# Attention with MLP on one core: the last 64 queries of all heads in one group of 128x64 column tiles per batch

## The chip, the cores and the metric

The kernel runs on one core of a Trainium2 chip. The metric is the device time of one execution in microseconds (us). TensorE is called PE, its weight loads PEld, VectorE DVE, ScalarE ACT, GpSimd POOL and SyncE SP, as in the profile.

## What is computed

Eight batches of eight heads with 576 tokens of width 64 go through causal attention with a decay that the gates s give, and the result, 512 wide, through a normalised two-layer MLP with a residual:

```python
cum = np.cumsum(np.maximum(s, 0.0), axis=-1)
bias = -(cum[:, :, :, None] - cum[:, :, None, :])
scores = np.where(causal, -1e9, scale * q @ k.T + np.minimum(bias, 0.0))
attn = softmax(scores)
x = (attn @ v).transpose(0, 2, 1, 3).reshape(B, S, H * D)
out = x + np.maximum(layer_norm(x) * g_ln @ w_ch1, 0.0) @ w_ch2
```

The inputs are float32, q, k and v of shape (8, 8, 576, 64); the weights are 512x2048 and 2048x512.

## The kernel before

The 576 tokens of a batch are four full blocks of 128 and a tail of 64 (`NF` = 4, `NT` = 5, `TL` = 64). Batches 0 and 1 run in an older form. From batch 2 on the work goes in pairs of heads, n = 4 b + j for batch b and pair j, and it is made of steps, each a short function:

- `burst(n)` (step `B2`, L541): the scores of two heads, transposed (keys in partitions, queries in columns). A head's q and k have 64 rows, so the two heads lie in the upper and the lower half of PE's rows and their matmuls alternate. Each head fills three banks of 512 columns: sa (key block 0, queries 0 to 511), sb (key block 0 with the tail queries, then key block 1), sc (key blocks 2 and 3). The six banks come from the PSUM pool "s" (six banks).
- `burst_exp` (`bx`, L551) on ACT takes the exponential of a bank into `er`, which has four slots, so heads h and h + 4 share one. `burst_mask` (`bm`, L560) on POOL zeroes the diagonal blocks. `tails`, `tails_exp`, `tails_mask` (`sd`, `se`, `sm`) make the scores of the tail's keys with the tail's queries of all eight heads of a batch, into `ed`; the tail's keys lie in `kz`.
- `pv_two(n, i)` (`Y`, L613): the product with v of one head. For each of five query blocks t the key blocks kb up to t are summed, which is 1 + 2 + 3 + 4 + 5 = 15 matmuls with 128x128 weights from `er` (or `ed` for the tail's keys) and 66 columns of v (64, and two with the weights of the sums). The tail has 64 queries, but its weights are 128 columns wide too, offset so that the 64 land in the lower half of the partitions in even batches and in the upper half in odd ones. The result `pot` takes a bank of the pool "m", which has two and also holds the MLP's `py`.
- `norm_two(n, i)` (`K`, L639) on DVE: sums, reciprocal, multiplication of the four full blocks into `xb`, and of the tail's 64 rows into `xm`, where the tails of two batches share a tile.
- `u` and `U`: quarters of the MLP of earlier batches, four matmuls of 512 columns each (`ph`, L761, and `py`, L780). `ga`, `la`, `La`, `Da` are the normalisation; `cr`, `lr`, `lv`, `tr`, `vm`, `vo` load and prepare q, k and v of later batches, the casts and weightings on POOL. The tails of all batches go through the MLP at the very end, as four mixed tiles of 128 rows.

The order of all steps on all engines is written out by hand, in a table of words (`PLAN`, L1278), such as `Y.19.0 B2.20`: each engine does its instructions in the order in which the words issue them. Waits between engines follow from who writes and reads what. A pool's bank is given to the next user in the order of the words, and the first instruction of that user waits until the last reader of the bank is done. Where PE's instructions wait, that stands at the weight load or the matmul, and all that follows on PE stands behind it.

The start matters in one place: POOL clears parts of `er` (L915) and then issues the loads of batch 1's v (L191), for which PE waits.

Of the kernel before, what the change touches and what calls it, by code (L numbers as in the profile page):

```python
# [9 lines left out]
F32 = mybir.dt.float32  # L10
# [6 lines left out]
P = 128  # L17
# [13 lines left out]
def fast_path(  # L31
# [26 lines left out]
    EW = 1664  # L58
# [7 lines left out]
    ET = H * TL + 2 * TL  # L66
# [50 lines left out]
    kz = const.tile([P, H * TL + TL], BF16, name="kz")  # L117
# [9 lines left out]
    ed = [c3f[:, i * ET : (i + 1) * ET] for i in range(2)]  # L127
    c_hi, c_mid, c_lo = (c3[0:BH, j, :] for j in range(3))
# [347 lines left out]
    def side_scores(b, j, i, banks):  # L476
# [51 lines left out]
    def ed_rows(b):  # L528
        return ed[b % 2][0:TL, TL : TL * (1 + H)].rearrange("p (h c) -> p h c", c=TL)
# [9 lines left out]
    BANKS = (("sa", 0, 0), ("sa", 1, 0), ("sb", 0, OB), ("sb", 1, OB), ("sc", 0, OC), ("sc", 1, OC))  # L539
# [11 lines left out]
    def burst_exp(n, x):  # L551
        name, i, o = BANKS[x]
        nc.scalar.activation(  # L553
            out=er[:, 2 * n % 4 + i, o : o + 512],
            in_=bank["B", n].pop((name, i)),
            func=ACT.Exp,
            scale=scale,
        )

    def burst_mask(n, x):  # L560
        o, step = ((0, OB + 64), (OC, 320))[x // 2]
# [30 lines left out]
    def pv_norm(b, h):  # L592
# [15 lines left out]
    TAIL_TWO = (  # L608
        (OB, OC - 64, OC + 256, OC + 448),
        (OB - 64, OC - 128, OC + 192, OC + 384),  # L610
    )

    def pv_two(n, i):  # L613
# [4 lines left out]
        pot = ptile("m", [P, NT, D2], "pot")  # L618
        for t in range(NT):
            for kb in range(t + 1):  # L620
                if kb == NF:
                    o = (h + 1 - b % 2) * TL
                    cols = ed[b % 2][:, o : o + P]
                else:
                    o = KOFF[kb] + t * P if t < NF else TAIL_TWO[b % 2][kb]
                    cols = e[:, o : o + P]
                nc.tensor.matmul(  # L627
                    pot[:, t, :],
                    lhsT=cols,
# [9 lines left out]
    def norm_two(n, i):  # L639
        b, h = n // NJ, 2 * (n % NJ) + i  # L640
        pot = pots.pop((n, i))
        rinv = rinvs[:, b, h, :]
        sums = small.tile([P, NT], F32, name="sums", tag="sums")
        nc.vector.tensor_reduce(out=sums, in_=pot[:, :, D:D2], axis=AX.X, op=ALU.add)  # L644
        nc.vector.reciprocal(out=rinv, in_=sums)
        hs = slice(h * D, (h + 1) * D)
        nc.vector.tensor_tensor(  # L647
            out=xb[b][:, :, hs],
            in0=pot[:, 0:NF, 0:D],
            in1=rinv[:, 0:NF].unsqueeze(2).to_broadcast([P, NF, D]),  # L650
            op=ALU.mult,
        )
        pr = tail_rows(b)
        nc.vector.tensor_scalar_mul(
# [921 lines left out]
```

## Time and profile before

| | us |
|---|---|
| median of 3 runs | 345.16 |
| runs | 344.2 to 345.6 |
| span of the profiled execution | 343.7 |
| PE busy in it | 333.9 |
| DVE, ACT, POOL busy | 207.1, 186.8, 168.7 |

The profile is of one execution. Its span runs from the first to the last instruction on record; the runs' times are taken around the whole execution, so that their median is 1.5 us above that span. A time of the profiled execution other than its span is not given. In the lists of groups a row names the source line, the engine, the operation, output and inputs with their shapes, the count, then behind the bar the busy time in us, the mean duration of one in ns, and the idle time before it with what ended it. In the timeline a row begins with the start and the length in us; rows of the same kind that follow each other are merged, and x14 is their number. A matmul's length is its latency (0.19 us for 66 columns); what it takes PE is the distance between two starts.

### The profile page before, as it was taken

The page shows a single profiled execution, that of the slowest core. Times are in us where ns is not written, and L with a number is a line of the kernel's source. Part 1 is how long each engine was busy: PE and PEld are TensorE (multiplying, and loading weights), DVE is VectorE, ACT ScalarE, POOL GpSimd, SP SyncE. Part 2 cuts the span into 40 slices and gives each one's busy share as a digit, 9 for nine tenths or more (in the row PEclk, how much of TensorE's full clock was granted, in tenths as well). Part 3 has the DMA queues.
Part 4 walks back from the last instruction along what each step waited for, and adds up shares of the span by engine and source line. Part 5 has one row for each costly group of instructions (what it writes and reads, how often), then busy time and mean ns, then how long its engine had stood idle before and what let it go on. Part 6 is the DMA issues. An engine that isn't in the chain of part 4 may idle for free.

```text
span 343.7 us, 8035 instructions
## 1 busy us (share of the span) xinstructions
PE 333.9 (97%) x3093; PEld 185.4 (54%) x3093; DVE 207.1 (60%) x589; ACT 186.8 (54%) x347; POOL 168.7 (49%) x306
## 2 busy tenths in 40 slices
PE   7999999899999999999999999999999999999994
PEld 2989765445545555555455555554555444444443
DVE  7688787937675787545753774557448624523412
ACT  4888899668755685448546864386344204202200
POOL 8997678876588766755684476441301001000000
PEclk9999999999999999999999999999999999999998
DMA  9999999799999999997687955600410141021022
GB/s 153 189 184 179 201 198 212 174 243 225 198 220 248 220 226 202 212 229 157 154 198 194 224 106 126 138 2 2 122 63 0 29 126 46 2 79 44 0 64 65
DMA packets 147962, 48.59 MB, mean 141 GB/s; under 512 B 135280, under 2 KB 143760, under 8 KB 147920
## 3 DMA queue, kind: packets, MB, share of 16 engines
q1 hardware_dynamic: 121856, 38.34, 51.4%
q0 software_dynamic: 24304, 8.92, 22.1%
q10 hardware_dynamic: 1760, 0.79, 0.9%
q8 instruction: 25, 0.41, 0.5%
q14 instruction: 17, 0.14, 0.1%
HBM read 37.11 MB, written 9.44 MB: 135 GB/s over the span
## 4 chain that ended last, share of the span: by engine, by line
PE 85%; POOL 7%; DVE 2%; DMA 2%; issue 1%; POOLq 0%
PE py L780 35%; PE ph L761 34%; PE pot L627 7%; DMA v_bf<-in_v_dram 2%; POOL v_bf L191 2%; PE sa L548 2%; POOL rowb L179 2%; PE sc L548 1%; PE sb L548 1%; PE pot L583 1%; DVE xn L710 1%; POOL w_bf L252 1%; POOL kq L910 1%; DVE yo L792 0%; DVE stats L669 0%
## 5 line engine op out<-in xcount | busy, mean ns | idle before, releaser
L780 PE MATMUL py<-w_bf,hT 128*128 128x512 bf16 (+2 forms) x608 | 130.9, 368 | 1.1 <-DVE yo L792 1.1
L761 PE MATMUL ph<-xT,w_bf 128*128 128x512 bf16 x480 | 109.8, 379 | 0.0
L752 ACT ACTIVATE hT<-ph 128x512 bf16<-128x512 f32 x102 | 61.2, 604 | 80.4 <-PE ph L761 78.8
L780 PEld LDWEIGHTS <-hT 128*128 128x128 bf16 x608 | 56.0, 98 | 61.4 <-issue 1.4
L761 PEld LDWEIGHTS <-w_bf 128*128 128x128 bf16 x544 | 51.0, 98 | 56.2
L492 POOL TENSOR_SCALAR_AFFINE_SELECT er<-er 128x256 bf16<-128x256 bf16 x96 | 37.5, 405 | 60.2 <-ACT er L553 45.1
L792 DVE SCALAR_TENSOR_TENSOR yo<-py,rstd,xb 128x512 f32<-128x512 f32 x32 | 24.0, 750 | 47.5 <-PE py L780 43.8
L553 ACT ACTIVATE er<-sb 128x512 bf16<-128x512 f32 x48 | 28.2, 609 | 21.7 <-PE sb L548 18.5
L750 DVE TENSOR_SCALAR hT<-ph 128x512 bf16<-128x512 f32 x34 | 23.4, 690 | 25.3 <-PE ph L761 24.6
L553 ACT ACTIVATE er<-sa 128x512 bf16<-128x512 f32 x48 | 28.6, 609 | 13.1 <-PE sa L548 10.2
L232 POOL TENSOR_TENSOR v_bf<-rowtmp,wt 128x512 bf16<-128x512 f32 (+1 forms) x30 | 33.8, 1134 | 2.8 <-DMA rowtmp<-in_v_dram 2.7
L553 ACT ACTIVATE er<-sc 128x512 bf16<-128x512 f32 x48 | 28.8, 613 | 5.4 <-PE sc L548 5.4
L627 PEld LDWEIGHTS <-er 128*128 128x128 bf16 x672 | 25.7, 97 | 9.5 <-issue 0.6
L627 PE MATMUL pot<-v_bf,er 128*128 128x66 bf16 x672 | 28.0, 193 | 0.0
L710 DVE SCALAR_TENSOR_TENSOR xn<-xb,mv,gb 128x512 bf16<-128x512 f32 x28 | 26.9, 960 | 1.0
L684 POOL TENSOR_TENSOR rstd<-rstd,mhalf 128x4 f32<-128x4 f32 (+1 forms) x8 | 8.8, 1094 | 36.9 <-DVE rstd L683 32.6
L644 DVE TENSOR_REDUCE sums<-pot 128x5 f32<-128x10 f32 x48 | 7.9, 165 | 30.0 <-PE pot L627 29.7
L669 DVE BATCH_NORM_STATS2 stats<-xb 128x6 f32<-128x128 f32 (+1 forms) x84 | 24.0, 323 | 0.4
L217 POOL CAST kq<-rowtmp 128x512 bf16<-128x512 f32 (+1 forms) x30 | 20.0, 681 | 6.3 <-DMA rowtmp<-in_k_dram 6.2
L647 DVE TENSOR_TENSOR xb<-pot,rinvs 128x256 f32<-128x256 f32 x48 | 20.4, 424 | 1.6
L548 PEld LDWEIGHTS <-kq 64*128 64x128 bf16 x360 | 11.2, 94 | 10.1 <-issue 4.7
L987 ACT ACTIVATE er<-st 128x512 bf16<-128x512 f32 x24 | 13.1, 603 | 1.8 <-PE st L978 1.8
(173 smaller groups left out, 398.3 us busy)
## 6 DMA issues: line engine op xcount, KB each, us to landing
out_dram<-yo SPq DMA_DIRECT2D x32, 256.0 KB
rowtmp<-in_v_dram SPq DMA_DIRECT2D x24, 256.0 KB
rowtmp<-in_k_dram SPq DMA_DIRECT2D x20, 256.0 KB
rowtmp<-in_q_dram SPq DMA_DIRECT2D x20, 256.0 KB
w_bf<-in_moe_w_ch_dram POOLq DMA_DIRECT2D x8, 512.0 KB, 9.2
kp<-in_k_dram POOLq DMA_DIRECT2D x8, 144.0 KB, 8.9
qp<-in_q_dram POOLq DMA_DIRECT2D x8, 144.0 KB, 8.9
v_bf<-in_v_dram POOLq DMA_DIRECT2D x8, 128.0 KB, 8.0
```

The lines of the kernel that those rows point to most:

```text
L232: e.tensor_tensor(out=v_bf[b % 2][0:pn, t, :, 0:D], in0=loaded.pop(("v", b, t))[0:pn], in1=wt[0:pn, t, b, :].unsqueeze(2).to_broadcast([pn ...
L492: nc.gpsimd.affine_select(out=out, in_=out, compare_op=ALU.is_ge, fill=0.0, base=0, pattern=pattern, channel_multiplier=-1,)
L548: nc.tensor.matmul(a, lhsT=lhsT, rhs=rhs, start=True, stop=True)
L553: nc.scalar.activation(out=er[:, 2 * n % 4 + i, o : o + 512], in_=bank["B", n].pop((name, i)), func=ACT.Exp, scale=scale,)
L627: nc.tensor.matmul(pot[:, t, :], lhsT=cols, rhs=v_bf[b % 2][:, kb, h, :], start=(kb == 0), stop=(kb == t),)
L669: nc.vector.bn_stats(out=st[b][:, t, part, :], in_=x_tiles(b)[t][:, lo:hi])
L710: nc.vector.scalar_tensor_tensor(out=xn, in0=tiles[t], scalar=mvs[b][:, t, 0:1] if b > 0 else mean0[:, t : t + 1], in1=gb, op0=ALU.subtrac ...
L750: nc.vector.tensor_scalar_max(out=dst, in0=ph, scalar1=0.0)
L752: nc.scalar.activation(out=dst, in_=ph, func=ACT.Relu)
L761: nc.tensor.matmul(ph, lhsT=w1_bf[:, kd, fb * P : (fb + 1) * P], rhs=xT[:, :, kd, :], start=(kd == 0), stop=(kd == KD - 1),)
L780: nc.tensor.matmul(py[t], lhsT=hT[:, fb, t * P : (t + 1) * P], rhs=w2_bf[:, fb, c0:c1], start=(fb == 0), stop=(fb == FB - 1),)
L792: nc.vector.scalar_tensor_tensor(out=yo, in0=py[t], scalar=rs, in1=x[:, c0:c1], op0=ALU.mult, op1=ALU.add)
```

## The change

In batches 2 to 7 the tail's queries are taken out of `pv_two`, which keeps 10 matmuls per head. A new step `Z` (`pv_tails`) multiplies the tails of all eight heads of a batch with v in one group: for each pair and each of five key blocks one matmul for each head, with 128x64 weights (the 64 tail columns alone), head 2j into partitions 0 to 63 and head 2j + 1 into partitions 64 to 127 of the same bank, so that the two are column tiles beside each other: 40 matmuls a batch. A new step `z` (`norm_tails`) normalises them with four DVE instructions. So that the tail columns of the first four heads live until `Z`, the slots of `er` grow to 1792 columns, and the bursts put the tail's queries at the bank's end for pairs 0 and 1, at its beginning for pairs 2 and 3. In batch 2 the burst's blocks are now cut at query 512, as they were already in later batches. `ed` loses its margins, and `kz` moves into the same buffer. The guard at the end gets two instructions.

`Z` stands before the first burst of the next batch, and `z` directly behind `Z`, ahead of that burst (in batch 7, without a next burst, behind the two last normalisations). In `PLAN`: in batches 4, 5 and 6 that is between the last two `Y` of the batch, in batch 7 behind both.

```diff
-    EW = 1664
+    EW = 1792
...
-    ET = H * TL + 2 * TL
+    ET = H * TL
+    EB, EC, ES = 512, 1152, 640
...
-    kz = const.tile([P, H * TL + TL], BF16, name="kz")
...
+    kz = c3f[:, 2 * ET : 3 * ET + TL]
...
+        full, tail = (0, 384) if j < NJ // 2 else (128, 0)
         add(banks["sa", i], 0, 0, 0, 512)
-        add(banks["sb", i], 0, 0, 512, 576)
-        add(banks["sb", i], 64, 1, 128, 576)
-        add(banks["sc", i], 0, 2, 256, 576)
-        add(banks["sc", i], 320, 3, 384, 576)
+        add(banks["sb", i], tail, 0, 512, 576)
+        add(banks["sb", i], full, 1, 128, 512)
+        add(banks["sb", i], tail + TL, 1, 512, 576)
+        add(banks["sc", i], full, 2, 256, 512)
+        add(banks["sc", i], tail, 2, 512, 576)
+        add(banks["sc", i], full + 256, 3, 384, 512)
+        add(banks["sc", i], tail + TL, 3, 512, 576)
...
-        pot = ptile("m", [P, NT, D2], "pot")
-        for t in range(NT):
+        pot = ptile("m", [P, NF, D2], "pot")
+        for t in range(NF):
...
+    def pv_tails(b):
+        pot = ptile("m", [P, NJ, D2], "pott")
+        for j in range(NJ):
+            lo = (EB + 512, EC + 512) if j < NJ // 2 else (EB, EC)
+            for kb in range(NT):
+                for i in range(2):
+                    h = 2 * j + i
+                    if kb == NF:
+                        cols = ed[b % 2][:, h * TL : (h + 1) * TL]
+                    else:
+                        o = lo[kb // 2] + kb % 2 * TL
+                        cols = er[:, h % 4, o : o + TL]
+                    nc.tensor.matmul(
+                        pot[i * TL : (i + 1) * TL, j, :],
+                        lhsT=cols,
+                        rhs=v_bf[b % 2][:, kb, h, :],
+                        start=(kb == 0),
+                        stop=(kb == NF),
+                    )
+        pots["t", b] = pot
+
+    def norm_tails(b):
+        pot = pots.pop(("t", b))
+        rinv = rinvs[:, b, 0:H:2, NF]
+        sums = small.tile([P, NJ], F32, name="sums", tag="sums")
+        nc.vector.tensor_reduce(out=sums, in_=pot[:, :, D:D2], axis=AX.X, op=ALU.add)
+        nc.vector.reciprocal(out=rinv, in_=sums)
         pr = tail_rows(b)
-        nc.vector.tensor_scalar_mul(
-            out=xm[b // 2][pr, hs], in0=pot[pr, NF, 0:D], scalar1=rinv[pr, NF : NF + 1]
-        )
+        for i in range(2):
+            r = slice(i * TL, (i + 1) * TL)
+            nc.vector.tensor_tensor(
+                out=xm[b // 2][pr].rearrange("p (j i d) -> p i j d", i=2, d=D)[:, i],
+                in0=pot[r, :, 0:D],
+                in1=rinv[r].unsqueeze(2).to_broadcast([TL, NJ, D]),
+                op=ALU.mult,
+            )
...
-    nc.gpsimd.memset(kz, 0.0)
-    nc.gpsimd.memset(rinvs[:, 0, :, NF], 1.0)
+    nc.gpsimd.memset(rinvs[:, :, :, NF], 1.0)
...
-        "me": lambda: [nc.gpsimd.memset(x, 0.0) for x in ed],
+        "me": lambda: nc.gpsimd.memset(c3f[:, 0 : 3 * ET + TL], 0.0),
...
-        u u U ga.4.0.3 bm.19.3 bx.19.4 bm.19.2 Y.18.0 u u ga.4.0.2 u K.18.0 ga.4.1.0 bm.19.0 Y.19.0 B2.20
+        u u U ga.4.0.3 bm.19.3 bx.19.4 bm.19.2 Y.18.0 u u ga.4.0.2 u K.18.0 ga.4.1.0 bm.19.0 Y.19.0 Z.4 z.4 B2.20
```

The clearing of `er` at the start (L915, `er[:, :, OD:EW]`) thereby covers 256 columns of each slot instead of 128. Below are PE's instructions at the end of batch 4, as they stand in the program (line, operation, output and inputs with the number of the buffer, shape; in brackets the semaphore it waits for, DVE_49 counting DVE's instructions, PE_49 PE's own). The first rows are of the kernel before: the last matmul of burst 20 and behind it the pot group `Y.19.1`, pot_3147, whose load waits for DVE.

```order
L548 LDWEIGHTS kq1_110
L548 MATMUL sc_3117<-kq1_110 128x64
L627 LDWEIGHTS er_117 [waits DVE_49]
L627 MATMUL pot_3147<-v_bf0_107,er_117 128x66 [waits PE_49]
L627 LDWEIGHTS er_117
```

The changed kernel at the same place: first the end of `Y.19.0` (pot_3077) and the beginning of `Z.4` (pott_3088), then, behind burst 20, `Y.19.1` (pot_3169).

```order
L626 MATMUL pot_3077<-v_bf0_107,er_116 128x66
L664 LDWEIGHTS er_116 [waits DVE_49]
L664 MATMUL pott_3088<-v_bf0_107,er_116 64x66 [waits PE_49]
L664 LDWEIGHTS er_116
L664 MATMUL pott_3088<-v_bf0_107,er_116 64x66
```

```order
L553 LDWEIGHTS kq1_110
L553 MATMUL sc_3139<-kq1_110 128x64
L626 LDWEIGHTS er_116 [waits DVE_49]
L626 MATMUL pot_3169<-v_bf0_107,er_116 128x66 [waits PE_49]
L626 LDWEIGHTS er_116
```

The load of `Y.19.1` waits for DVE in both. Before, the value was that of the normalisation of `Y.18.0`, which stands before `Y.19.0`; now `Z.4` has taken that bank, and the value is that of the last multiplication of `z.4`. DVE's rows there, before (pot_3054 is `Y.18.0`, pot_3147 `Y.19.1`, pot_3096 `Y.19.0`):

```order
L647 TENSOR_TENSOR xb_2652<-pot_3054,rinvs_115 128x4x64 [waits DVE_49]
L654 TENSOR_SCALAR xm2_120<-pot_3054,rinvs_115 64x64
L669 BN_STATS stats_2958<-xb_2652 128x6 [waits DVE_49]
L669 BN_STATS stats_2958<-xb_2652 128x6
L644 TENSOR_REDUCE sums_3163<-pot_3147 128x5 [waits PE_49]
L645 RECIPROCAL rinvs_115<-sums_3163 128x5 [waits DVE_49]
L647 TENSOR_TENSOR xb_2652<-pot_3147,rinvs_115 128x4x64 [waits DVE_49]
L654 TENSOR_SCALAR xm2_120<-pot_3147,rinvs_115 64x64
L644 TENSOR_REDUCE sums_3168<-pot_3096 128x5
```

And now:

```order
L700 BN_STATS stats_2951<-xb_2669 128x6 [waits DVE_49]
L677 TENSOR_REDUCE sums_3129<-pott_3088 128x4 [waits PE_49]
L678 RECIPROCAL rinvs_114<-sums_3129 128x4 [waits DVE_49]
L682 TENSOR_TENSOR xm2_119<-pott_3088,rinvs_114 64x4x64 [waits DVE_49]
L682 TENSOR_TENSOR xm2_119<-pott_3088,rinvs_114 64x4x64
L700 BN_STATS stats_2951<-xb_2669 128x6
L643 TENSOR_REDUCE sums_3180<-pot_3169 128x4 [waits PE_49]
L644 RECIPROCAL rinvs_114<-sums_3180 128x4 [waits DVE_49]
L645 TENSOR_TENSOR xb_2669<-pot_3169,rinvs_114 128x4x64 [waits DVE_49]
L643 TENSOR_REDUCE sums_3184<-pot_3077 128x4
```

`Y.19.0`'s own normalisation (pot_3077) still stands behind that of `Y.19.1`, so its bank is not free before, and the tails' four instructions have come between. Batches 5 and 6 have the same order. At the end of batch 7 PE went from the last pot group (pot_4740, `Y.31.0`) to the MLP:

```order
L627 MATMUL pot_4740<-v_bf1_108,er_117 128x66
L627 LDWEIGHTS c3_123
L627 MATMUL pot_4740<-v_bf1_108,c3_123 128x66
L761 LDWEIGHTS w1_bf_99
L761 MATMUL ph_4769<-xT_1340,w1_bf_99 128x512
```

Now `Z.7` (pott_4719) stands directly behind `Y.31.0` (pot_4708) and takes the same bank, while the other still holds `Y.31.1`; its first load waits for DVE's multiplication of pot_4708:

```order
L626 MATMUL pot_4708<-v_bf1_108,er_116 128x66
L664 LDWEIGHTS er_116 [waits DVE_49]
L664 MATMUL pott_4719<-v_bf1_108,er_116 64x66 [waits PE_49]
L664 LDWEIGHTS er_116
L664 MATMUL pott_4719<-v_bf1_108,er_116 64x66
```

More of the change, by code (lines that the diff above doesn't have):

```diff
@@ L606, in pv_norm @@
         )
[L608 to L611 removed]
+    MAIN = (0, EB, EC - P, EC)
     def pv_two(n, i):
@@ L641, in norm_two @@
         pot = pots.pop((n, i))
-        rinv = rinvs[:, b, h, :]
-        sums = small.tile([P, NT], F32, name="sums", tag="sums")
+        rinv = rinvs[:, b, h, 0:NF]
+        sums = small.tile([P, NF], F32, name="sums", tag="sums")
         nc.vector.tensor_reduce(out=sums, in_=pot[:, :, D:D2], axis=AX.X, op=ALU.add)
         nc.vector.reciprocal(out=rinv, in_=sums)
-        hs = slice(h * D, (h + 1) * D)
         nc.vector.tensor_tensor(
-            out=xb[b][:, :, hs],
-            in0=pot[:, 0:NF, 0:D],
-            in1=rinv[:, 0:NF].unsqueeze(2).to_broadcast([P, NF, D]),
+            out=xb[b][:, :, h * D : (h + 1) * D],
+            in0=pot[:, :, 0:D],
+            in1=rinv.unsqueeze(2).to_broadcast([P, NF, D]),
@@ L1159, in guard @@
             )
+        nc.vector.tensor_tensor(
+            out=key[TL:P, NOLD:, 0:H:2, NF],
+            in0=rinvs[TL:P, NOLD:, 0:H:2, NF],
+            in1=wt[TL:P, NF, NOLD:, 1:H:2],
+            op=ALU.mult,
+        )
         nc.vector.scalar_tensor_tensor(
```

48 lines of the change are left out of this document (24 added, 24 removed).

## Prediction

> **What bounds the kernel now.** I read the page first, then TensorE's waits, then its timeline around the places that the change touches. The page's first two parts:
>
> ```profile
> PE 333.9 (97%) x3093; PEld 185.4 (54%) x3093; DVE 207.1 (60%) x589; ACT 186.8 (54%) x347; POOL 168.7 (49%) x306
> ...
> PEclk9999999999999999999999999999999999999998
> ```
>
> TensorE (PE) is busy 97% of the span and its granted clock is full in all slices but the last. Between 72 us, where the two-heads stage has begun, and 324 us, where only the end is left, the windows view gives (length; then busy us and counts of PE, weight loads, DVE, ACT, POOL; clock; DMA):
>
> ```profile
> 72.00:324.00 252.00, 252.00 (x2081) 128.47 (x2079) 146.33 (x422) 129.93 (x242) 110.59 (x205) 1.00 0.62 135
> ```
>
> PE never idles there, and the waits view lists no wait of a matmul in it; all of batches 2 to 7 lies in it. So the time is a sum of what PE is given to do. A shorter group is won in full, a new wait of PE is lost in full, and work moved off DVE, ACT or POOL is worth nothing by itself. The timeline of PE where batch 4 ends (start, length, then the group):
>
> ```profile
> 156.62 0.58 PE L627 MATMUL pot<-v_bf,er 128*128 128x66 bf16 x14
> 157.04 0.19 PE L627 MATMUL pot<-v_bf,c 128*128 128x66 bf16 x1
> 157.16 0.39 PE L548 MATMUL sa<-kq 64*128 64x512 bf16 x2
> 157.39 0.38 PE L548 MATMUL sb<-kq 64*128 64x64 bf16 x6
> 157.61 0.39 PE L548 MATMUL sc<-kq 64*128 64x256 bf16 x8
> 157.93 0.60 PE L627 MATMUL pot<-v_bf,er 128*128 128x66 bf16 x14
> 158.37 0.19 PE L627 MATMUL pot<-v_bf,c 128*128 128x66 bf16 x1
> 158.39 1.03 PE L761 MATMUL ph<-xT,w_bf 128*128 128x512 bf16 x4
> ```
>
> Three prices are in it. **A pot matmul:** 14 steps from 156.62 to 157.04, 0.030 us each. **A change of tile mode:** from the last pot matmul to the burst 0.12 us instead of 0.03, so 0.09. **Two tiles side by side:** the burst has 1536 columns for each head. The four 512-column matmuls at 158.39 start 0.216 apart ((1.03 - 0.38) / 3), so 1536 columns are 0.65 us; the whole burst, both heads, took 157.16 to 157.93, 0.77. Take off the mode change at its end and 0.03 is left over for 8 pairs: the second head cost about 0.004 per pair.
>
> **The change, part by part.**
>
> *Removed:* 5 of the 15 matmuls of each of 48 groups: 240 x 0.030 = **-7.20 us**.
>
> *Added:* 240 matmuls of as many columns (66) with 64-column weights, in 120 pairs on the two column tiles. No such matmul is in the trace. If a pair runs as the burst's pairs do, it costs 0.030 to 0.034; if the two take turns, 0.060. Their weight loads must keep up, too. Weight loads of few columns are in the trace once, in the start, beside the burst's (groups by shape, behind the bar busy us and mean ns; then two stretches of the timeline):
>
> ```profile
> L275 PEld LDWEIGHTS <-c 96*64 96x64 bf16 x3 | 0.2, 108 | 0.1
> L627 PEld LDWEIGHTS <-er 128*128 128x128 bf16 x672 | 25.7, 97 | 9.5 <-issue 0.6
> ...
> 12.49 0.14 PEld L275 LDWEIGHTS <-c 96*64 96x64 bf16 x2
> ...
> 80.00 0.11 PEld L548 LDWEIGHTS <-kq 64*128 64x128 bf16 x4
> ```
>
> A load of 64 columns lasts longer (108 ns) than one of 128 (97), and two of them into the same tile start about 0.03 us apart (0.14 less 0.108). The burst's four loads, two for each of two tiles, all start within 0.02 us (0.11 less 0.094). So a narrow load takes about 0.028 us, just under a matmul's 0.030, and hides behind the matmul before it if tiles load side by side as the burst's do. I take 0.032 for a pair, since the burst is the nearest row: 120 x 0.032 = **+3.84 us**; ends 3.6 and 7.2.
>
> The Trainium skill, TensorEngine Tiling (Array Packing), Restrictions, says that column tiling rules out the fast weight load, and TensorE: Matmul & The Clock Gate, LDWEIGHTS, prices a plain load at its columns divided by 1.2 per ns. By that, an estimate, 64 columns are 0.053 us, a pair could not be shorter even side by side, and the sum below would come to +2.8 us, 347.9. The trace agrees that the narrow load is the slow kind, but has it at 0.03.
>
> *Mode changes.* Batches 2 to 6 get one more (into column tiles; the one into the burst was there), batch 7 one on the way out, its way in lying in a wait, below. That a narrow group costs the same is seen once, at the guard's matmul with one-column weights:
>
> ```profile
> 323.93 0.59 PE L761 MATMUL ph<-xTm,w_bf 128*128 128x512 bf16 x2
> 324.45 0.20 PE L1185 MATMUL count<-count,ones 128*1 128x8 f32 x2
> 324.58 0.39 PE L780 MATMUL py<-w_bf,hT 128*128 128x512 bf16 x1
> ```
>
> Its first pass should have come at 324.36 (323.93 and two steps of 0.216) and came 0.09 later. 6 x 0.09 = **+0.54 us**; from 0 to twice that.
>
> *New waits.* The pool "m" has two banks, and now three users. In batches 4, 5 and 6 the tails' group stands between the last two pot groups, with nothing but a burst behind it: one bank holds a pot that is normalised later, so the next pot takes the tails' bank and waits for the last of four DVE instructions, as DVE's and PE's rows in the section on the change show. In batch 7 the tails' group itself waits, for the pot just made. What the chain on DVE takes is seen at the end of batch 7 (PE, then DVE; and two rows for the forms that come in):
>
> ```profile
> 262.17 0.19 PE L627 MATMUL pot<-v_bf,c 128*128 128x66 bf16 x1
> 262.20 0.38 PE L761 MATMUL ph<-xT,w_bf 128*128 128x512 bf16 x1
> ...
> 262.40 0.17 DVE L644 TENSOR_REDUCE sums<-pot 128x5 f32<-128x10 f32 x1 [0.35 <-PE pot L627]
> 262.60 0.19 DVE L645 RECIPROCAL rinvs<-sums 128x5 f32<-128x5 f32 x1
> 262.83 0.42 DVE L647 TENSOR_TENSOR xb<-pot,rinvs 128x256 f32<-128x256 f32 x1
> ...
> L1051 DVE TENSOR_TENSOR xm<-pot,rinvs 64x256 f32<-64x256 f32 x2 | 0.8, 417 | 0.1
> ...
> 155.53 0.42 DVE L647 TENSOR_TENSOR xb<-pot,rinvs 128x256 f32<-128x256 f32 x1
> 155.87 0.27 DVE L654 TENSOR_SCALAR xm<-pot,rinvs 64x64 f32<-64x64 f32 x1
> 156.06 0.47 DVE L669 BATCH_NORM_STATS2 stats<-xb 128x6 f32<-128x128 f32 x2
> 158.60 0.17 DVE L644 TENSOR_REDUCE sums<-pot 128x5 f32<-128x10 f32 x1 [2.07 <-PE pot L627]
> ...
> 65.03 0.76 DVE yo L792
> 65.83 1.89 PE py L780 x8
> ```
>
> From a group's last matmul to the multiplication's start is 0.66 us (262.17 to 262.83). The tails have two of 64x256, 0.42 each, the second 0.34 behind the first (as at 155.53 and 155.87): 0.66 + 0.34 + 0.42 = 1.42, and PE starts 0.04 after DVE ends (65.79 to 65.83), so 1.46. DVE is free then (idle from 156.53 to 158.60). PE's own way from that last matmul over the burst to the next pot is 0.89 (157.04 to 157.93). PE waits 0.57, three times: +1.71. In batch 7 the multiplication ends at 263.25, PE would start at 263.29 instead of 262.20: +1.09. Behind the waiting load stands all of PE's order. **+2.80 us**; from 1.2, were the mode change and the chain to overlap better, to 3.5. In batches 2 and 3 at least three groups of four 512-column matmuls (4 x 0.216 us each) stand between, and no wait comes.
>
> *At nothing.* DVE loses 48 small multiplications and gets 24 instructions; PE never waited for them, and where it does now is counted:
>
> ```profile
> L654 DVE TENSOR_SCALAR xm<-pot,rinvs 64x64 f32<-64x64 f32 x48 | 13.4, 279 | 0.5
> ```
>
> Batch 2's bursts are cut into three more pairs each, of the same columns: 12 x 0.004 = +0.05 us. The guard's two extra instructions and the exponentials' new offsets lie beside PE. No DMA is moved. On DVE the statistics of the mixed tail tile move behind the tails' normalisation; PE needs what comes of them only for the mixed chunk, the ph<-xTm group that ends at 323.93.
>
> *The start.* POOL clears twice as much of er before it issues batch 1's v, and PE waits for that v:
>
> ```profile
> 19.67 0.53 POOL L915 MEMSET er<- 128x512 bf16 x1
> ...
> 24.50 4.24 POOL L191 DMA_DIRECT2D v_bf<-in_v_dram  x5
> ...
> 35.86 0.60 PE L583 MATMUL pot<-v_bf,er 128*128 128x65 bf16 x6 [0.42 <-DMA v_bf<-in_v_dram]
> ```
>
> The clearing grows by up to 0.53 us; the transfers take 8 us in busy queues and may swallow it. Between 0 and 0.53 I take **+0.2 us**.
>
> Sum: -7.20 + 3.84 + 0.54 + 2.80 + 0.05 + 0.20 = **+0.2 us**, span 343.7 to 343.9. The runs shown lie at 344.2 to 345.6, median 345.16, 1.5 above that span; with the same distance, **345.4 us**. A measurement of this kernel tells about 0.5%, 1.7 us, from no change.
>
> **Rivals.**
>
> *The tiles take turns* (slower). The place is each pair; it decides as soon as the two loads, 0.028 each, or the two matmuls, 0.030 each, cannot run at once. Then a pair is 0.058, 120 are 6.96, and the sum is +3.3: **348.5**. For it: both column tiles draw on all 128 rows, while the burst's two tiles have 64 rows each, so the burst is no proof, and the change then does not do what it says. Against: the burst's loads and matmuls of two tiles start within 0.004 of each other.
>
> *Every load is laid bare.* Load and matmul in turn, 0.028 + 0.030 for each of 240: 13.9, sum +10.3, **355.5**. Against it: the 15 pot matmuls follow each other at 0.030 although each has its own load over the same rows. The Trainium skill, TensorE: Matmul & The Clock Gate, Part 3, says that a load overlaps a running matmul only where the row groups differ, which would give this case; the trace disagrees for full-width tiles at 0.030.
>
> *The waits are hidden* (faster). If DVE's chain ended before the burst does, or the banks were handed out otherwise, 2.8 us come back: **342.6**. Against: 1.42 against 0.89, and the order of the rows.
>
> **How the numbers follow.** Forecast 0.64, turns 0.26, laid bare 0.04, hidden waits 0.06. The forecast's own range, by its bounds (pair 0.030 to 0.036, waits 2.2 to 3.3, start 0 to 0.5), is 344.4 to 346.4. The whole range takes in the turns with theirs: 344.3 to 349.0. Faster by over 0.5%: the hidden waits and a little of the forecast, 0.08; within: 0.60; slower: the turns, the bare loads and the forecast's edge, 0.32.
>
> **What would show it.** A tails' group from its first matmul to the burst of 0.65 to 0.75 us (40 matmuls) and pairs that start within 0.004: the forecast; 1.2 to 1.3: turns; over 2: bare loads. Waits of PE for DVE's tail multiplication of about 0.6 us in three places and of 1.1 us in batch 7, where PE had none. The forecast is wrong if PE's 15-matmul groups do not shrink to 0.30 us, or if waits appear at other places.

## The result, and the profile after

The changed kernel took **351.51 us** (median of 6 runs, 350.57 to 352.38), the kernel before beside it 345.68 (344.2 to 347.41). The ratio is 1.0161, with a 95% interval of 1.0131 to 1.0191. It is slower by some 5.8 us. The prediction said 345.4, with a range of 344.3 to 349.0: too low, and the time lies outside the range. (Of the twelve runs of a_best, below, two of 348.5 and 348.9 us fell into a slower state of the chip and are left out of its median.)

The profiled execution has a span of 350.2 us, 6.5 above that of before. Its page and its windows view (length; busy us and counts of PE, weight loads, DVE, ACT, POOL; clock; DMA), over the stretch that answers to 72 to 324 us before:

```profile
PE 329.9 (94%) x3093; PEld 182.3 (52%) x3117; DVE 204.2 (58%) x568; ACT 186.7 (53%) x347; POOL 167.2 (48%) x304
...
72.00:330.00 258.00, 252.11 (x2111) 127.63 (x2130) 143.39 (x404) 131.40 (x246) 111.37 (x207) 1.00 0.67 135
```

PE's busy time fell by 4 us, its share from 97% to 94%. In the two-heads stage, where it never idled, it now stands still for 5.9 of 258 us. What it waits for is in the waits view, of the changed kernel and then of the kernel before (who waits, for whom; us in total, times, longest):

```profile
PE py L811 <- DVE yo L823: 2.9, 2, 1.6
PE pot L626 <- DVE xm L682: 1.8, 3, 0.6
PE ph L1102 <- issue: 1.5, 1, 1.5
...
PE pot L1058 <- DVE kq L143: 1.4, 1, 1.4
...
PE pott L664 <- DVE xb L645: 0.9, 1, 0.9
```

```profile
PE py L780 <- DVE yo L792: 1.1, 1, 1.1
...
PE pot L583 <- DMA v_bf<-in_v_dram: 0.4, 1, 0.4
```

The second and the last of the five are the forecast's waits for a bank. The other three were not forecast. Most of them lies ahead of any column tile: the wait without a releaser at 34 us, that for kq at 42 and the larger of the two for yo, at 69 (the kernel before has one of 1.1 us there). Where the first two-heads burst stands, the changed kernel is already 3.4 us late (burst 8 begins at 73.03 us, before at 69.64).

**The tails' group itself** did what the forecast said. PE's timeline in batch 4, then DVE's:

```profile
160.67 0.46 PE L626 MATMUL pot<-v_bf,er 128*128 128x66 bf16 x10
161.06 0.32 PE L664 MATMUL pott<-v_bf,er 128*64 128x66 bf16 x8
...
161.69 0.20 PE L664 MATMUL pott<-v_bf,c 128*64 128x66 bf16 x2
161.82 0.39 PE L553 MATMUL sa<-kq 64*128 64x512 bf16 x2
...
163.26 0.47 PE L626 MATMUL pot<-v_bf,er 128*128 128x66 bf16 x10 [0.61 <-DVE xm L682]
163.57 0.59 PE L792 MATMUL ph<-xT,w_bf 128*128 128x512 bf16 x2
```

```profile
161.93 0.17 DVE L677 TENSOR_REDUCE sums<-pott 128x4 f32<-128x8 f32 x1 [1.46 <-PE pott L664]
162.13 0.18 DVE L678 RECIPROCAL rinvs<-sums 128x4 f32<-128x4 f32 x1
162.34 0.86 DVE L682 TENSOR_TENSOR xm<-pott,rinvs 64x256 f32<-64x256 f32 x2
```

From its first matmul (161.06) to the burst (161.82) the group of 40 takes 0.76 us, 0.10 of it the change of mode: 0.033 a pair. A pot group takes 0.31 (163.26 to 163.57). The multiplications end at 163.20, and PE goes on at 163.26. The group is 0.01 us above the stretch that the prediction named as the forecast's sign (0.65 to 0.75), and far from that of the turns (1.2 to 1.3).

**The start.** DVE, POOL and PE around 40 us in the changed kernel:

```profile
36.73 0.77 DVE L143 COPY kq<-trqk 64x576 bf16<-64x576 bf16 x1
39.72 0.20 DVE L602 RECIPROCAL rinvs<-pot 128x5 f32<-128x5 f32 x1 [2.22 <-POOL rinvs L965]
...
41.87 0.80 DVE L143 COPY kq<-trqk 64x576 bf16<-64x576 bf16 x1
```

```profile
38.67 0.78 POOL L256 DMA_DIRECT2D w_bf<-in_moe_w_ch_dram  x1
39.45 0.24 POOL L965 MEMSET rinvs<- 128x64 f32 x1
```

```profile
42.72 0.76 PE L1058 MATMUL pot<-v_bf,er 128*128 128x65 bf16 x20 [1.44 <-DVE kq L143]
```

L965 sets the tail reciprocals to one. It did so for batch 0 and now does for all batches, so batch 1's first normalisation (L602) writes a place that L965 writes too, and has to wait for it. L965 stands behind POOL's loads. DVE stands still for 2.2 us with the next copy into kq (41.87) behind, and PE waits for that copy.

**Batch 2.** DVE, then POOL, in the changed kernel; then POOL and DVE at the same place before:

```profile
98.89 0.17 DVE L677 TENSOR_REDUCE sums<-pott 128x4 f32<-128x8 f32 x1 [1.46 <-PE pott L664]
...
101.24 4.46 DVE L741 SCALAR_TENSOR_TENSOR xn<-xb,mv,gb 128x512 bf16<-128x512 f32 x1
...
105.88 0.98 DVE L741 SCALAR_TENSOR_TENSOR xn<-xb,mv,gb 128x512 bf16<-128x512 f32 x1
```

```profile
99.73 2.03 POOL L233 TENSOR_TENSOR v_bf<-rowtmp,wt 64x512 bf16<-64x512 f32 x2 [2.90 <-DMA rowtmp<-in_v_dram]
...
103.56 1.03 POOL L233 TENSOR_TENSOR v_bf<-rowtmp,wt 128x512 bf16<-128x512 f32 x1
104.55 0.60 POOL L218 CAST rowb<-rowtmp 128x512 bf16<-128x512 f32 x1
105.11 1.21 POOL L497 TENSOR_SCALAR_AFFINE_SELECT er<-er 128x256 bf16<-128x256 bf16 x2
```

```profile
96.06 3.05 POOL L232 TENSOR_TENSOR v_bf<-rowtmp,wt 64x512 bf16<-64x512 f32 x2 [2.67 <-DMA rowtmp<-in_v_dram]
```

```profile
96.01 0.75 DVE L710 SCALAR_TENSOR_TENSOR xn<-xb,mv,gb 128x512 bf16<-128x512 f32 x1
```

DVE stood idle for 1.46 us, until the tails' group was done, with the statistics of batch 2 behind `z.2`. The first xn then began while POOL was at work, and lasted 4.46 us where the shortest of its kind take 0.75: it ended within the two masks at 105.11, which took 1.21 us together where two take 0.76 elsewhere, so that here POOL was held up. Before, xn (96.01) came just ahead of POOL's weighting of v (96.06), and it was POOL whose instructions took longer (1.5 to 1.6 us each instead of 1.0). The output yo stands behind xn, and PE waits for it at 107.9 and 110.2 us.

### The profile page after: what moved, and what is told of

Read it like the earlier page. It is cut to its first block, busy times and chain, and to the rows that moved or that the text cites. A ratio compares the mean times of both kernels' runs of the same rounds, so it can differ in the third digit from the quotient of the medians.

```text
span 350.2 us, 8036 instructions
## 1 busy us (share of the span) xinstructions
PE 329.9 (94%) x3093; PEld 182.3 (52%) x3117; DVE 204.2 (58%) x568; ACT 186.7 (53%) x347; POOL 167.2 (48%) x304
## 4 chain that ended last, share of the span: by engine, by line
PE 78%; DVE 8%; POOL 6%; DMA 5%; issue 2%; POOLq 0%
PE ph L792 33%; PE py L811 32%; DMA v_bf<-in_v_dram 5%; PE pot L626 5%; DVE xn L741 2%; PE sa L553 2%; PE pott L664 1%; POOL v_bf L192 1%; PE sc L553 1%; PE sb L553 1%; PE pot L590 1%; DVE xm L682 1%; DVE stats L700 1%; POOL rowb L180 1%; DVE yo L823 1%
## 5 line engine op out<-in xcount | busy, mean ns | idle before, releaser
L811 PE MATMUL py<-w_bf,hT 128*128 128x512 bf16 (+2 forms) x584 | 128.8, 367 | 4.7 <-DVE yo L823 2.9
L497 POOL TENSOR_SCALAR_AFFINE_SELECT er<-er 128x256 bf16<-128x256 bf16 x96 | 38.6, 417 | 50.3 <-ACT er L560 35.9
L233 POOL TENSOR_TENSOR v_bf<-rowtmp,wt 128x512 bf16<-128x512 f32 (+1 forms) x30 | 32.4, 1087 | 3.1 <-DMA rowtmp<-in_v_dram 2.9
L741 DVE SCALAR_TENSOR_TENSOR xn<-xb,mv,gb 128x512 bf16<-128x512 f32 x28 | 28.5, 1018 | 1.0
L626 PEld LDWEIGHTS <-er 128*128 128x128 bf16 x480 | 19.8, 97 | 11.7 <-DVE xm L682 2.3
L626 PE MATMUL pot<-v_bf,er 128*128 128x66 bf16 x480 | 22.1, 193 | 2.2 <-DVE xm L682 1.8
L218 POOL CAST kq<-rowtmp 128x512 bf16<-128x512 f32 (+1 forms) x30 | 19.1, 651 | 10.5 <-DMA rowtmp<-in_k_dram 10.5
L643 DVE TENSOR_REDUCE sums<-pot 128x4 f32<-128x8 f32 x48 | 7.8, 162 | 24.3 <-PE pot L626 23.9
L218 POOL CAST rowb<-rowtmp 128x512 bf16<-128x512 f32 (+1 forms) x20 | 12.1, 614 | 6.0 <-DMA rowtmp<-in_k_dram 5.1
```

The source lines that it names most:

```text
L218: nc.gpsimd.tensor_copy(out=rows[b % 2][0:pn, t, u], in_=loaded.pop(("kq"[u], b, t))[0:pn])
L233: e.tensor_tensor(out=v_bf[b % 2][0:pn, t, :, 0:D], in0=loaded.pop(("v", b, t))[0:pn], in1=wt[0:pn, t, b, :].unsqueeze(2).to_broadcast([pn ...
L497: nc.gpsimd.affine_select(out=out, in_=out, compare_op=ALU.is_ge, fill=0.0, base=0, pattern=pattern, channel_multiplier=-1,)
L626: nc.tensor.matmul(pot[:, t, :], lhsT=e[:, o : o + P], rhs=v_bf[b % 2][:, kb, h, :], start=(kb == 0), stop=(kb == t),)
L741: nc.vector.scalar_tensor_tensor(out=xn, in0=tiles[t], scalar=mvs[b][:, t, 0:1] if b > 0 else mean0[:, t : t + 1], in1=gb, op0=ALU.subtrac ...
L811: nc.tensor.matmul(py[t], lhsT=hT[:, fb, t * P : (t + 1) * P], rhs=w2_bf[:, fb, c0:c1], start=(fb == 0), stop=(fb == FB - 1),)
```

## The experiments

Time is the median; the ratio is against runs of the kernel before on the same chip. The last two columns are read from each profile, which is of one execution: PE's wait at the copy into kq (about 41 us) and its waits for yo in batch 2 (106 to 112 us). The intervals of a_er, a_banks and a_z2 overlap that of the changed kernel, so what these three say rests on their profiles more than on their medians.

| run | us (runs) | ratio, 95% | kq | yo |
|---|---|---|---|---|
| changed kernel | 351.51 (6) | 1.0161, 1.0131 to 1.0191 | 1.4 | 1.3 and 0.4 |
| a_rinvs | 349.28 (6) | 1.0105, 1.0078 to 1.0131 | none | as the changed |
| a_er | 350.99 (6) | 1.0140, 1.0108 to 1.0171 | 1.5 | none |
| a_banks | 350.54 (6) | 1.0142, 1.0111 to 1.0173 | 1.3 | as the changed |
| a_z2 | 350.30 (5) | 1.0149, 1.0123 to 1.0174 | 1.5 | none |
| b_rinvs (on before) | 349.34 (6) | 1.0108, 1.0072 to 1.0145 | 2.1 | none |
| a_all | 344.22 (12) | 0.9965, 0.9941 to 0.9989 | none | none |
| a_all_er | 345.61 (12) | 0.9999, 0.9973 to 1.0024 | none | none |
| a_best | 344.65 (10) | 0.9987, 0.9962 to 1.0011 | none | none |
| a_pool | 350.15 (1) | | 1.4 | 0.8 and 0.4 |
| a_serial | 352.67 (1) | | none | as the changed |

**a_rinvs**

```diff
-    nc.gpsimd.memset(rinvs[:, :, :, NF], 1.0)
+    nc.gpsimd.memset(rinvs[:, 0, :, NF], 1.0)
+    nc.gpsimd.memset(rinvs[:, 2:B, :, NF], 1.0)
```

> The changed kernel with one edit: POOL's setting of the tail reciprocals of all batches to one is split, batch 0 as before and batches 2 to 7 in an instruction of its own behind it, so that the first normalisation of batch 1 no longer writes what that instruction writes. Theory (the wait is real): DVE's first reciprocal of batch 1 starts as soon as its pot is there, no longer at the end of the setting (39.72 us), PE's wait of 1.4 us for the copy into kq at about 41 goes, and the first two-heads burst comes 1.6 to 2.3 us earlier than in the changed kernel (73.0), so 349.2 to 349.9 by the median against 351.5. Rival (the start is bound by its loads, and the wait only hides the next one): the burst stays within 0.5 us of 73.0 and the time at 351 to 352.

DVE's timeline:

```profile
35.44 0.77 DVE L143 COPY kq<-trqk 64x576 bf16<-64x576 bf16 x1
36.88 0.20 DVE L602 RECIPROCAL rinvs<-pot 128x5 f32<-128x5 f32 x1 [0.67 <-PE pot L590]
```

The reciprocal now waits for its pot and no longer for POOL. PE's waits at 41 and at 69 us are gone, and burst 8 begins at 68.99, 4.0 us earlier. That is more than the 1.6 to 2.3 expected, because the stall at 33 us (1.5 us), which this edit has nothing to do with, did not come in this execution either. Of the 4.0, 2.0 were given back up to burst 12, in waits for POOL's masks and tail keys; 1.9 stay from burst 14 on, and the median is 2.2 lower, as expected. The theory holds.

**b_rinvs**, the same instruction put into the kernel before:

```diff
-    nc.gpsimd.memset(rinvs[:, 0, :, NF], 1.0)
+    nc.gpsimd.memset(rinvs[:, :, :, NF], 1.0)
```

> The kernel before with one edit: POOL sets the tail reciprocals of all batches to one there, in one instruction, instead of those of batch 0 alone. Nothing else differs, and no column tile is in it. Theory: DVE's first normalisation of batch 1 now waits for POOL, PE's wait of about 1.5 us for the copy into kq appears at 40 us where there was none, and the time is 346.8 to 347.6 against 345.3. Rival (the wait needs the later loads of the changed kernel as well): PE's new wait is under 0.5 us and the time stays at 345 to 346.

PE's waits, and windows behind the first of them (the clock is the third number from the end):

```profile
PE pot L1028 <- DVE kq L142: 2.1, 1, 2.1
PE py L780 <- DVE yo L792: 1.6, 1, 1.6
```

```profile
41.00:42.00 1.00, 1.00 (x24) 1.00 (x24) 0.58 (x3) 0.00 (x0) 0.00 (x0) 0.68 1.30 198
42.00:43.00 1.00, 1.00 (x9) 0.56 (x7) 0.74 (x4) 0.13 (x1) 0.00 (x0) 0.50 1.26 192
...
45.00:46.00 1.00, 1.00 (x16) 0.79 (x14) 0.97 (x3) 0.36 (x2) 1.00 (x2) 1.00 1.25 207
```

This one instruction, without any column tile, makes the kernel before 3.8 us slower, more than expected. The wait is there, 2.1 us (DVE's reciprocal begins at 37.96, where POOL's setting has ended at 37.93), and behind it PE's granted clock is at 0.50 to 0.68 for over 3 us, so that most of the wait is paid again. All bursts of the profile lie 3.1 us later than before. In the profile of a_er the same wait (1.5 us) is followed by the same drop, from 42 to 46 us; in those of the changed kernel, a_banks, a_z2 and a_pool it is not.

**a_er**

```diff
-    nc.gpsimd.memset(er[:, :, OD:EW], 0.0)
+    nc.gpsimd.memset(er[:, :, OD : OD + P], 0.0)
```

> The changed kernel with one edit: the clearing of er at the start takes 128 columns of each slot again instead of 256. Theory (the clearing delays POOL's loads, and what PE waits for lands later): POOL's loads of batch 1's v are issued 0.4 us earlier, the stall of PE at about 33 us (1.7 us, with no semaphore behind it) is gone or shorter, and 0.4 to 1.4 us come back: 350.1 to 351.1. Rival (that stall is PE's own instruction supply, late by the load of the DMA queues, and has nothing to do with the 0.4 us): the stall stays at 1 to 2 us or turns up at another place, and the time stays at 351 to 352.

The stall at 33 us is gone and PE is 1.7 us ahead at 39 us, but the drop of the clock behind the wait at 41 takes all of that, and burst 8 comes at 72.98. The median is 0.5 lower, within the spread: this run does not decide what the clearing costs. The stall at 33 us (row "issue": the instruction waits for nothing that the profile shows) is not the clearing's: it is missing as well in six other profiles with 256 columns (a_rinvs, a_banks, a_z2, a_pool, a_serial, a_one), and came again, at 0.5 us, in a_all_er, which has 256, and in a_best, which has 128. The traces speak for the rival, PE's instruction supply. The stall comes at the same instruction of PE in all three profiles. Queue 8 (kind "instruction") moves 16 KB at a time, 25 times in the changed kernel, about once for every 250 of PE's instructions, so it is taken for PE's supply; its last transfer ahead of that instruction began at 31.5 to 32.2 us in these three and at 29.2 to 30.9 in the ten others. Why it began late is open.

**a_all_er**, the same question without the other waits: a_all (below) with 256 columns.

> The kernel with all four edits, but with the clearing of er at the start over 256 columns again. Theory (the 0.4 us later issue of batch 1's v costs PE more than that, since its five loads then land later in full queues: PE's waits for v at 35 to 38 us summed 0.6 to 2.8 us in the six runs with 256 columns, and 0 to 0.9 in the four with 128): waits for v of 0.8 us or more at 35 to 38 us, and a time 0.4 to 1.2 us above the 344.2 with 128 columns. Rival (later waits swallow it): the waits come back, but the time stays within 0.3 us.

The median is 1.4 us above that of a_all, the intervals overlap a little. The waits for v that the theory named did not come in the profiled execution; what came is the wait for yo at 67 us (1.6 us, none in a_all) and the stall of 0.5 us. So the clearing probably costs about a microsecond, and not in the place that I gave; by what way is not shown.

**a_banks**: PE's order stays, DVE's changes.

```diff
-Y.19.0 Z.4 z.4 B2.20 ... Y.19.1 K.19.1 K.19.0
+Y.19.0 K.19.0 Z.4 z.4 B2.20 ... Y.19.1 K.19.1
...
-Y.31.1 U bm.31.0 ga.7.1.2 u Y.31.0 Z.7 K.31.0 K.31.1 z.7
+Y.31.1 U bm.31.0 K.31.1 ga.7.1.2 u Y.31.0 Z.7 K.31.0 z.7
```

(batches 5 and 6 in the same way)

> The changed kernel with an edit of the order on DVE alone: the normalisation of the pot group ahead of the tails' group stands right behind that group in batches 4 to 7, not behind the next one, so that the next user of the pool takes its bank and not the tails'. PE's order is unchanged. Theory (the four waits are waits for a bank): PE's waits for DVE's last tail multiplication (three of 0.67 us) and of the tails' group in batch 7 (1.0 us) fall below 0.1 us each, and 3.0 us come back: 348.5. Rival (what PE waits for there is DVE being late as such): the waits only change their names, and less than 1 us comes back.

PE's timeline where batch 4 ends:

```profile
163.67 0.39 PE L553 MATMUL sa<-kq 64*128 64x512 bf16 x2
...
164.44 0.47 PE L626 MATMUL pot<-v_bf,er 128*128 128x66 bf16 x10
```

The pot group follows the burst's beginning after 0.77 us instead of 1.44, with no wait. The three waits are gone (bursts 21, 25 and 29 close up by 0.61 to 0.63 us each), and of the one in batch 7 half is left (0.4). The profile gains 2.4 us in all there. The median fell by 1.0 only: this profile's start lost 0.8 us in waits for v, and 1.1 more went up to burst 18. The waits were waits for a bank; of that in batch 7 this run shows it for half, and a_all, where the normalisation stands earlier still, has none.

**a_z2**

```diff
-Y.11.1 K.11.1 ... ga.2.1.0 u Z.2 z.2 B2.12
+Y.11.1 Z.2 K.11.1 z.2 ... ga.2.1.0 u B2.12
```

> The changed kernel with one edit: in batch 2 the tails' group and its normalisation stand right behind the last pot group, two units of the MLP earlier. Theory (in the changed kernel DVE sits idle for 1.7 us before the tails' normalisation, with the statistics and xn behind it, xn then starts while POOL works without a gap and takes 4.46 us instead of 0.75 to 1.3, and PE waits 1.7 us for what follows): DVE's xn of batch 2 start 1.5 us or more earlier in relation to the burst, none lasts over 2.5 us, PE's waits for yo at about 107 and 110 go, and 1.3 to 1.9 us come back: 349.6 to 350.2. Rival (xn is slow wherever it falls on POOL's casts, and the batch's POOL work sets the pace): an xn of over 3 us and a wait of PE of over 1 us remain, and the time stays at 351 to 352.

DVE's timeline:

```profile
96.63 0.17 DVE L677 TENSOR_REDUCE sums<-pott 128x4 f32<-128x8 f32 x1
...
99.17 1.40 DVE L741 SCALAR_TENSOR_TENSOR xn<-xb,mv,gb 128x512 bf16<-128x512 f32 x1
...
100.75 2.18 DVE L741 SCALAR_TENSOR_TENSOR xn<-xb,mv,gb 128x512 bf16<-128x512 f32 x1
```

DVE does not stand idle for the tails, no xn lasts over 2.2 us, and the waits for yo are gone: burst 14 comes 2.0 us earlier relative to burst 13. Of this 1.2 us came back by burst 18, in waits for the transposed xn (DMA) and a mask (POOL); the median is 1.2 lower.

One profile does not prove the edit, for the waits for yo are missing in a_er too, where batch 2 is as in the changed kernel and DVE stands idle for the tails as long (1.46 us). There xn just got through; in a_serial, below, one that began at the same time did not (xn of a_er, then of a_serial):

```profile
101.91 0.91 DVE L741 SCALAR_TENSOR_TENSOR xn<-xb,mv,gb 128x512 bf16<-128x512 f32 x1
```

```profile
101.91 4.37 DVE L741 SCALAR_TENSOR_TENSOR xn<-xb,mv,gb 128x512 bf16<-128x512 f32 x1
```

POOL's weighting ahead of it began at 100.23 and at 100.27. So late behind `z.2` an xn usually falls into POOL's work, and now and then slips past. Over all profiles the edit stands: PE waits for yo in batch 2 in six of the seven with `z.2` where the change put it, and in none of the four with `z.2` moved (a_z2, a_all, a_all_er, a_best).

**a_pool**: the tails' normalisation stays ahead of xn, POOL's order changes.

```diff
-bx.12.5 bm.12.3 vm.3.3:P cr.4.1.0 ga.2.2.2 bx.12.3 bm.12.1 u bx.12.2 bm.12.0
+bx.12.5 bm.12.3 ga.2.2.2 bx.12.3 bm.12.1 u bx.12.2 bm.12.0 vm.3.3:P cr.4.1.0
```

> The changed kernel with an edit of the order on POOL alone: in batch 2 one weighting of v and one cast of the rows stand behind the next two masks instead of ahead of them, so that POOL has gaps (it waits for exponentials) while DVE works on xn. PE's and DVE's orders are unchanged, and the tails' normalisation still stands ahead of xn. Theory (DVE's xn stands still while POOL goes from one instruction to the next without a gap): the xn at about 101 us, 4.46 us long, becomes 1 us or more shorter, and PE's wait for yo at 107.9 (1.44) shrinks by as much. Rival (its length is that of DVE's own inputs or of its lateness behind the tails' normalisation): it stays over 4 us.

```profile
99.88 2.62 DVE L741 SCALAR_TENSOR_TENSOR xn<-xb,mv,gb 128x512 bf16<-128x512 f32 x1
...
102.67 2.36 DVE L741 SCALAR_TENSOR_TENSOR xn<-xb,mv,gb 128x512 bf16<-128x512 f32 x1
```

The first xn is 1.8 us shorter with nothing changed on DVE or PE, so its length hangs on POOL's order. But the second is 1.4 longer, and the wait fell by 0.5 us only: POOL's work was moved from the one onto the other.

**a_serial** and **a_one** test the pairs.

```diff
-            for kb in range(NT):
-                for i in range(2):
+            for i in range(2):
+                for kb in range(NT):
```

> The changed kernel with one edit: the loops of the tails' group are turned, so that the five matmuls of one head come one behind the other and then the five of its neighbour; the two column tiles no longer alternate. Theory (a pair runs side by side only while the two tiles alternate): the 40 matmuls, 0.66 us in the changed kernel, take 1.1 to 1.25 us, and the time rises by 6 x 0.5 = 3 us less what the waits hide. Rival (the halved weights alone make a matmul cheap, whatever the order): the group stays below 0.8 us.

```profile
161.68 0.34 PE L664 MATMUL pott<-v_bf,er 128*64 128x66 bf16 x7
161.83 0.20 PE L664 MATMUL pott<-v_bf,c 128*64 128x66 bf16 x1
```

My theory failed: from first to last start the group takes 0.69 us, against 0.63 in the changed kernel. The first matmul on `c` (161.83) is the fifth of the first head, with four on `er` ahead of it; seven on `er` have begun by then, so three of the second head's run already beside it. (There is no wait for kq in this profile although L965 is as in the changed kernel: DVE waited for POOL even longer, 3.9 us, but PE had waited for v and then ran at a granted clock of 0.50 from 38 to 41 us, and came to the place later. a_one's profile has the same drop.)

So a_one put all of it on one tile:

```diff
-                        pot[i * TL : (i + 1) * TL, j, :],
+                        pot[0:TL, j, :],
```

> The changed kernel with all 40 matmuls of the tails' group put into the one column tile of partitions 0 to 63, head after head as in the run with the turned loops; the tails of the even heads are then not what they should be, and both tail multiplications read the lower half. It tells why the turned loops cost only 0.06 us a group. Theory (the two tiles work on their own, so that five matmuls of one run beside the five of the other, whatever the order of issue): on one tile the matmuls follow each other at 28 to 30 ns and the group takes 1.1 to 1.25 us from its first to its last start, against 0.63 and 0.69. Rival (a matmul with 64 weight columns takes half the time by itself): it stays at 0.6 to 0.75 us.

With these tails the guard at the end takes the kernel's general path, so that the whole time (5884 us) says nothing of the group. PE's timeline of it in batch 4:

```profile
162.16 0.31 PE L664 MATMUL pott<-v_bf,er 128*64 128x66 bf16 x4
...
162.35 0.29 PE L664 MATMUL pott<-v_bf,er 128*64 128x66 bf16 x4
...
162.50 0.29 PE L664 MATMUL pott<-v_bf,er 128*64 128x66 bf16 x4
```

Five matmuls take 0.16 us, 0.031 each, and the group 1.26 us. Narrow weights do not make a matmul cheaper; the second tile does. And the tiles need not alternate: five matmuls of one run beside five of the other.

**a_all**: a_rinvs, a_er, a_z2 and a_banks together, and in batch 7 `K.31.1` directly behind `Y.31.1`.

> The changed kernel with four edits together: the setting of the tail reciprocals split as in the run before, the clearing of er back to 128 columns, the tails' group of batch 2 behind the last pot group, and the normalisation ahead of the tails' group moved forward in batches 4 to 7 (in batch 7 ahead of the MLP unit too). Theory (the new waits are of the order and the setting, not of the column tiles): of the changed kernel's waits in the two-heads stage none of DVE's tail multiplication stays, and those of about 41, 69, 107 and 110 us are gone; the last burst, at 254.3 us in the changed kernel, comes at 247 to 250, and the time is 343.5 to 346, level with the kernel before (345.3). Rival (the waits only move on, as two thirds of a microsecond or more came back elsewhere in each run so far): waits on POOL's masks, the tail keys or the transposed xn take their place with over 2 us together, and the time is 347 or more.

Two rows of PE's waits view and the windows view of the stretch:

```profile
PE pot L626 <- POOL er L497: 1.0, 1, 1.0
PE sd L524 <- POOL c L145: 0.9, 1, 0.9
```

```profile
72.00:323.00 251.00, 249.11 (x2093) 125.53 (x2091) 140.31 (x401) 128.16 (x240) 109.98 (x205) 1.00 0.67 135
```

344.22 us, 0.35% below the kernel before (interval 0.11% to 0.59%). All waits of the change are gone, and against the changed kernel 7.3 us: the column tiles were not what cost. The theory holds (the last burst comes at 248.1). Two waits took their place, 1.9 us by those rows. Behind both stands a load: POOL's copy of the tail keys waits for the transposing transfer of kq, and its masks stand behind casts that wait for a transfer of k.

**a_best** moves those two: the scores of batch 3's tails two units later, and three masks ahead of the casts.

```diff
-bm.11.3 u sd.3 U bm.11.1 u se.3
+bm.11.3 u U bm.11.1 u sd.3 se.3
...
-cr.5.4.0 u cr.5.4.1 bx.17.2 bx.17.3 ... cr.5.2.0 bm.17.1 tr.5.4.5 bx.17.5 bm.17.3 ... lv.5.4 bm.17.0
+cr.5.4.0 u bx.17.2 bx.17.3 bm.17.1 bm.17.0 bx.17.5 bm.17.3 cr.5.4.1 ... cr.5.2.0 tr.5.4.5 ... lv.5.4
```

> The kernel with all four edits and two more of the order: in batch 2 the scores of batch 3's tails, whose keys came 1.09 us too late for PE, stand two MLP units later; in batch 4 three masks stand on POOL ahead of casts that wait for a transfer, since PE waited 1.12 us for the last of them. Theory (these two waits are of the order on POOL and PE, and PE has work in hand to fill them): both fall below 0.3 us, no other of over 0.5 us comes between 72 and 324 us, and the time is 342.0 to 343.5, against 344.2 with four edits and 345.6 before. Rival (PE has caught up with the loads of the next batches there, so that every earlier start ends in the next wait for a transfer): waits of as much come at the next place that needs a load, and the time stays at 343.8 to 344.8.

```profile
PE pot L590 <- DMA v_bf<-in_v_dram: 1.0, 3, 0.4
PE ph L792 <- DMA xT<-xn: 1.0, 1, 1.0
...
PE pot L626 <- POOL er L497: 0.5, 1, 0.5
```

344.65 us: not better than a_all. The two waits are gone and others stand in their place, for the transposed xn at 114.7 us and a mask at 151.5, ahead of which POOL had worked without a gap since a wait for a load (0.9 us, up to 145.4). The time and the new waits are those of the rival, that PE has caught up with what the transfers deliver there; that it holds for every such place is not shown.

## Why the prediction was wrong, point by point

- **What bounds the kernel.** PE was the bound, and every new wait of PE in the two-heads stage was indeed lost. But I read "PE never idles" as "nothing else is near". DVE, POOL and the transfers were only just ahead: PE's work shrank by 2.7 us by the terms of the next point, and waits for DVE, POOL and transfers ate more than that. With the waits of the change removed, a_all gains 1.3 us and no more, and a_best suggests why: what is won is waited for at the next transfer or mask. Waits at other places than the forecast's were its own sign of being wrong, and they came.
- **Pot matmuls, pairs, mode changes.** Right. Removed -7.20; the six groups cost 6 x 0.66 = 3.9 (forecast 3.84) and their mode changes 0.10 each (0.09). The rivals of tiles in turn and of bare loads are out: a_one shows what turns would have cost, 1.26 us a group. That a pair takes 0.032 was carried over from the burst, whose tiles lie otherwise, and came out right. Against the estimate by the Trainium skill, TensorE: Matmul & The Clock Gate, LDWEIGHTS (0.053 us at least for a pair), a pair took 0.033.
- **New waits.** The mechanism was right and a_banks shows it. Measured are 0.67 three times (from the burst to the pot group 1.44 us in the changed kernel, 0.77 in a_banks) and 1.0: 3.0 us, forecast 2.8.
- **"DVE loses 48 small multiplications and gets 24 instructions; PE never waited for them".** Failed, in batch 2. The prediction asked there whether a bank comes late, and not what stands behind `z.2` on DVE while it waits for PE. It was the statistics and xn, and xn came into POOL's work. This cost 1.3 and 0.4 us at PE in the profile; with `z.2` moved it is gone.
- **"The guard's two extra instructions [...] lie beside PE", and the start at +0.2.** Failed, and the costliest. The line that sets all reciprocals to one was in the diff, and had no term: its 0.24 us lie beside PE, but the prediction did not ask whose writes now overlap with it. With its later effects it is worth 2.2 us in the changed kernel and 3.8 in the kernel before. The clearing of er grew by 0.43 us (0.53 to 0.96), which the term of 0.2 took up; by a_all and a_all_er it probably costs about 1 us.
- **The sum.** -7.2 + 3.9 + 0.6 + 3.0 is +0.3, close to the forecast's first terms; the start (3.4 by burst 8) and batch 2 (1.8) make it 5.5 of the span's 6.5. Of the 3.4, 1.5 are the stall at 33 us, which came in this profile and, at 0.5, in only two of the twelve others. The last 1.0 us I cannot place; it lies in pieces below half a microsecond. One slip stands in the prediction's ranges: by its bounds the forecast's own range ends at 346.7, not 346.4.

## What to carry to other kernels

A clearing or setting that is widened can cost more than its own length: ask which later writes it now overlaps, on which engine, and what that engine's next instructions are waited for. An instruction that is put into an engine's order and waits there delays all that stands behind it, and may push it into another engine's work. Where one engine is busy all the time, the others may be only just ahead; shortening its work by 2.7 us was worth 1.3 us here, and only after four further edits.

## What the runs showed of the hardware

- **A wait of PE can be paid twice.** In a_er and b_rinvs a wait of 1.5 and 2.1 us was followed by a granted clock of about one half for over 3 us; in four other profiles the same wait was not. In a_serial and a_one waits for v of 1.6 and 1.9 us together were followed by the same drop, in a_banks 2.3 us of them were not. The Trainium skill, TensorE: Matmul & The Clock Gate, Part 1, has a half-rate clock that is decided in free-running windows of 3.4 us. The length of the drop agrees (b_rinvs lost 0.32, 0.50, 0.50 and 0.39 of four microseconds, at half rate 3.4 us), and windows that run freely would explain why the same wait has it only in some executions. But the page names a whole idle window for it, and here 1.5 us idle was enough.
- **A DVE instruction can be passed over by POOL many times.** The xn of 4.46 us began at 101.24 and ended at 105.70, while POOL went through six instructions that began in that time up to 104.55, and only the mask at 105.11 was held up. The Trainium skill, SBUF — State Buffer, SBUF: two separate sides, has an exclusive lock that the first of the two holds for its whole instruction. If it is this lock that xn waited for, which the profile does not say, it did not get it at the end of that instruction. Which of the two comes first can hang on hundredths of a microsecond: the xn of a_er and a_serial, 0.91 and 4.37 us long, both began at 101.91, and POOL's weighting ahead of them at 100.23 and 100.27.
- **Column tiles need no alternating order**: 0.69 us with five matmuls of a head in a row, 0.63 alternating, 1.26 on one tile.
